# Linear attention and two MLPs on one core: eight slots for input weights, out weights laid out by result

## The chip, the cores and the metric

The program runs on one core of one Trainium2 chip. The metric is its time on the chip in microseconds (us), as the median of several runs. TensorE (PE) multiplies, ScalarE (ACT), VectorE (DVE) and GpSimd (POOL) work on elements, SyncE (SP) issues most of the transfers.

## The reference, cut to what matters

Four batches of eight heads, 576 positions, head size 64: linear attention, then two MLPs over the 2304 tokens, all with a model size of 512. In the kernel's inputs the values are 64 bits wide; the kernel turns the weights into 32-bit numbers itself.

```python
def phi(x):
    proj = np.einsum('bhsd,df->bhsf', x, w_phi)               # 64 -> 128
    proj = proj - np.max(np.abs(proj), axis=-1, keepdims=True)
    return np.concatenate([np.exp(proj), np.exp(-proj)], axis=-1)
kv = np.einsum('bhsf,bhsd->bhfd', phi(k), v)
attn = (phi(q) @ kv) / (phi(q) @ z + 1e-06)                   # z: sum of phi(k)
x = attn                                                      # 2304 x 512
h = x @ w_in                                                  # 512 -> 2048
x = np.maximum(0.01 * h, h) @ w_out                           # 2048 -> 512
g = x @ w_gate                                                # 512 -> 1536
out = (g * (1 / (1 + np.exp(-g))) * (x @ w_val)) @ w_out2     # 1536 -> 512
```

## The kernel before, in words

**Products.** Each factor of a product is split into a high and a low part, and a product is three matmuls: high by high, high by low, low by high. A weight tile is 128 x 2 x 512: 512 columns of the high part and 512 of the low one. Results stand in four PSUM banks ("pm"), 128 x 288 each, half of a batch's 576 tokens.

**Units.** The MLPs are cut into 297 units, in order of the batches 0 to 3 (`units`). In the first two batches a unit is 24 matmuls (two halves of 12): `u_l1` (one 128-wide block f of the first MLP's 2048 columns), `u_gate` and `u_val` (the same for the second MLP's 1536), and `u_out`. `u_out(kind, b, c, o)` multiplies four blocks of such columns (a chunk c of `CH` = 4) by the out weights and adds the product to result block o, one of four (`KD`). A chunk's four `u_out` follow when its blocks are there. The addition on VectorE (L883) frees the PSUM bank. In the third batch's first MLP (`seven_beside`) and in the whole fourth batch (`seven`) two first-layer products are made with seven block products where eight are usual (class `Quad`), and `u_out` comes in halves beside them.

**Weights.** A weight tile has a key (kind, batch, number); the kinds are "1" (w_in), "2" (w_out), "g", "v" and "3" (w_out2). In the first batch a key is a raw 64-bit load of 512 KB into a slot of tag "wi" (`w_load`, L675; five slots of 4 KB a partition), a conversion to 32 bits into tag "wr" (four slots; `f32_steps`, ScalarE L691 to L697, VectorE L701 to L719), and a split into a high and a low part (`to_wtile`: ScalarE L737, VectorE L78). The split tile of a first-layer key is in "wi" too, that of an out key in "wo" (five slots). Results are stored to memory: 32-bit weights as `kept` (SyncE, L725), split out weights as `parts` (by GpSimd's queue, L773, 28 of them). The second batch loads `kept` again and splits again, the later ones load `parts` (L656). In the fourth batch the out tile whose number is 3 modulo 4 has a slot of its own ("vhl").

**What sets the order.** The lists `need` and `after` say when a key is due: a first-layer key has its slot four units ahead of the unit that needs it, an out key right after the unit that makes the columns it multiplies. `order` is the list of all keys by slot. For each key `split_next` (L1228) loads two keys past those done, converts one past, splits one, and then loads on up to `depth()` keys past those done: 5, or 4 where a key of batch 1 is near. All loads stand in SyncE's queue, where one that has no slot yet holds back those behind it.

**Attention.** That of the first batch is the opening, an order written out by hand (`OPENING`, some 450 names; CG3 and CG2 are steps of the conversion of the third kind of the first four weights, KP11 a product of the keys, XL7 the last result's low part). At KP2 in it the first four raw weights are loaded. The attention of each later batch is spread over the units of the one before. A scheduler of the language makes the final order of each engine of all this.

The out weights of key ("2", b, f) before are rows 128 f to 128 f + 127 of w_out, for all four results: the 512 columns of its tile are four blocks o of 128, and `u_out` takes block `oc` of four tiles.

Of the kernel before, what the change touches and what calls it, by code (L numbers as in the profile page):

```python
# [60 lines left out]
def linear_attention_two_mlps(ctx: ExitStack, tc, qT, kT, vt, w_phi, w1, w2, wg, wv, w3, cst, out):  # L61
# [573 lines left out]
    def parts_tile(key):  # L635
        tag = ("wi", 5)
# [21 lines left out]
    def w_load(key, tag="wi", n=5):  # L658
# [6 lines left out]
        elif (kind, f) in parts and second_of_pair(key):  # L665
            d = parts[kind, f].rearrange("p (a k n) -> p a k n", a=2, k=2)
            tag = ("wr", 4) if kind == "1" else ("wi", 5)
# [88 lines left out]
    def w_split(key):  # L756
# [20 lines left out]
        if kind == "1":  # L777
# [5 lines left out]
            for name, x in (("1X", even), ("1Y", r)):  # L783
                t = T([P, 2, 512], F32R, "wi", 5)
                to_wtile(t, x)
                unkept.append(((name, f // 2), t))
# [284 lines left out]
    after = {}  # L1071
# [17 lines left out]
    def seven(kind, b):  # L1089
# [5 lines left out]
        def o():  # L1095
            if not queue:
                return lambda: None
            (k, bb, c, last), oo, t = queue.pop(0)
            return lambda: u_out(k, bb, c, oo, last, (t,))

        def all_of(*fns):
            return lambda: [fn() for fn in fns]

# [10 lines left out]
        for m in range(n):  # L1114
# [15 lines left out]
            if kind == "1":  # L1130
                for f in range(4 * m, 4 * m + 4):
                    after.setdefault(end, []).append(("2", b, f))
                held.append(("1", b, m, m == n - 1))
            elif m % 2:
                for f in range(2 * m - 2, 2 * m + 2):
                    after.setdefault(mid, []).append(("3", b, f))
# [9 lines left out]
    def seven_beside(b):  # L1146
# [4 lines left out]

        def o():
            (k, bb, c, last), oo, t = queue.pop(0)
            return lambda: u_out(k, bb, c, oo, last, (t,))

        def two(*fns, w=()):
            return unit(lambda: [fn() for fn in fns], w)
# [4 lines left out]
        for m in range(NF1 // 4):  # L1162
# [10 lines left out]
            places = [two(y.p5, more[1]), two(more[2], more[3])]  # L1173
            two(more[4], more[5])
            places.append(two(more[6], y.p3))
            end = two(more[7], y.p4, w=[("1", b, 4 * m + 3)])
            places.append(end)
            for k in range(4):
                after.setdefault(places[k] if m == 0 else end, []).append(("2", b, 4 * m + k))
# [5 lines left out]
    for b in range(QB):  # L1185
        first = len(units)
        for f in range(NF1 if b != QA else 0):
            unit(lambda b=b, f=f: u_l1(b, f), [("1", b, f)])
            flush()
            after.setdefault(len(units) - 1, []).append(("2", b, f))  # L1190
# [6 lines left out]
        for f in range(NF2):  # L1197
# [3 lines left out]
            after.setdefault(len(units) - 1, []).append(("3", b, f))  # L1201
# [9 lines left out]
    for i in range(NU):  # L1211
        for k in need[i]:
            slots[max(-1, i - 4)].append(k)
        slots[i] += after.get(i, [])
# [138 lines left out]
```

## Time and profile before

| | |
|---|---|
| median of 3 runs | 1054.92 us (1054.34 to 1055.16) |
| the profiled execution | 1054.82 us |
| its span, first to last instruction | 1052.9 us |
| TensorE busy, matmuls | 1036.7 us, 98% |
| VectorE busy | 793.5 us, 75% |
| ScalarE busy | 650.5 us, 62% |
| GpSimd busy | 21.4 us, 2% |

The profile is one execution. Busy is the time in which an engine has an instruction in work; matmuls overlap each other, so that a busy share says when TensorE stands still, and not how well it is used. A line such as L816 is a line of the kernel; `pm<-gp,wo` reads: tile pm written from tiles gp and wo.

### The profile page before, as it was taken

To read this page: it belongs to the slowest core of one execution; us is meant where nothing else is said; L and a number is where in the kernel's file an instruction comes from. 1 tells how busy PE (TensorE), PEld (TensorE's weight loads), DVE (VectorE), ACT (ScalarE), POOL (GpSimd) and SP (SyncE) were. 2 spreads that over 40 slices of the span, in tenths; PEclk is the share of its full clock that TensorE was granted. 3 is DMA by queue.
4 is the path that set the end of the run, shared out by engine and by line. 5 is a ranking of instruction groups with operands and counts; after the bars stand their busy time and mean duration, and the time that the engine had idled before them with its cause. 6 is when DMAs were issued, how large, how long until landed. Compare 5 with 4: busy or idle time off the path is not lost.

```text
span 1052.9 us, 20402 instructions
## 1 busy us (share of the span) xinstructions
PE 1036.7 (98%) x7638; PEld 1016.8 (97%) x7638; DVE 793.5 (75%) x1726; ACT 650.5 (62%) x1448; POOL 21.4 (2%) x57
## 2 busy tenths in 40 slices
PE   9999999999999999999999999999999999999998
PEld 7899999999999999999999989999999999999998
DVE  6988888998999799678676766868778632468464
ACT  6879887898977788456543667735443244336431
POOL 1001100000000000000000000000000000000000
PEclk9999999999999999999999999999999999999999
DMA  8239777577765998765535486356886777558542
GB/s 267 60 129 309 274 264 263 168 248 217 261 192 200 356 339 284 285 230 192 192 120 189 134 319 243 141 203 217 291 285 237 272 267 264 183 167 297 191 145 76
DMA packets 101489, 236.16 MB, mean 224 GB/s; under 512 B 19856, under 2 KB 35984, under 8 KB 101392
## 3 DMA queue, kind: packets, MB, share of 16 engines
q1 hardware_dynamic: 95888, 219.74, 60.3%
q0 software_dynamic: 4032, 14.68, 3.6%
q8 instruction: 60, 0.98, 0.4%
q10 hardware_dynamic: 1472, 0.46, 0.2%
q14 instruction: 37, 0.30, 0.1%
HBM read 169.30 MB, written 65.54 MB: 223 GB/s over the span
## 4 chain that ended last, share of the span: by engine, by line
PE 83%; DVE 6%; ACT 5%; DMA 4%; issue 1%; SPq 0%; POOL 0%; DVEq 0%; ACTq 0%; POOLq 0%
PE pm L816 55%; PE pa L942 9%; PE pm L942 5%; PE pa L459 5%; PE pa L248 2%; PE pa L260 2%; PE pa L207 2%; DMA wi<-in_w_dram 2%; ACT wr L691 1%; DMA wr<-kept 1%; ACT wi L694 1%; ACT gp L90 1%; DVE gp L78 1%; PE pm L518 1%; DVE wr L701 1%
## 5 line engine op out<-in xcount | busy, mean ns | idle before, releaser
L816 PE MATMUL pm<-xh,wi 128*128 128x288 f32 x1664 | 350.5, 298 | 1.4 <-ACT wi L737 1.2
L816 PE MATMUL pm<-gp,wo 128*128 128x288 f32 x2256 | 338.4, 296 | 2.8 <-DVE acc L883 2.3
L816 PEld LDWEIGHTS pm<-gp,wo 128*128 128x128 f32 x2256 | 311.9, 188 | 4.8 <-DVE acc L883 3.0
L816 PEld LDWEIGHTS pm<-xh,wi 128*128 128x128 f32 x1664 | 271.1, 188 | 3.2 <-ACT wi L737 1.4
L816 PE MATMUL pm<-xl,wi 128*128 128x288 f32 x832 | 246.2, 297 | 0.0
L816 PEld LDWEIGHTS pm<-xl,wi 128*128 128x128 f32 x832 | 156.1, 188 | 0.8
L883 DVE TENSOR_TENSOR acc<-pm,acc 128x288 f32<-128x288 f32 x160 | 70.0, 452 | 47.2 <-PE pm L816 46.4
L78 DVE TENSOR_TENSOR gp<-es,gp 128x576 fp32r<-128x576 f32 x94 | 70.6, 752 | 31.8 <-ACT gp L90 31.0
L90 ACT ACTIVATE gp<-es 128x576 fp32r<-128x576 f32 x94 | 64.8, 694 | 29.9 <-DVE es L864 24.9
L78 DVE TENSOR_TENSOR wi<-wr,wi 128x512 fp32r<-128x512 f32 x96 | 64.7, 683 | 12.1 <-ACT wi L737 11.5
L737 ACT ACTIVATE wi<-wr 128x512 fp32r<-128x512 f32 x92 | 58.0, 643 | 25.6 <-PE pm L816 10.8
L942 PE MATMUL pm<-xh,wi 128*128 128x288 f32 x272 | 62.6, 297 | 1.8 <-DMA wi<-parts 1.6
L78 DVE TENSOR_TENSOR fl<-ff,fh 128x512 fp32r<-128x512 f32 (+1 forms) x72 | 50.9, 712 | 12.1 <-ACT fh L90 11.8
L691 ACT ACTIVATE wr<-wi 128x512 f32<-128x512 f32 x68 | 47.9, 704 | 17.0 <-DMA wi<-in_w_dram 7.8
L719 DVE TENSOR_TENSOR wr<-wr,wi 128x512 uint16<-128x512 uint16 x68 | 51.1, 754 | 0.8
L942 PEld LDWEIGHTS pm<-xh,wi 128*128 128x128 f32 x272 | 46.3, 188 | 2.9 <-DMA wi<-parts 1.8
L694 ACT ACTIVATE wi<-wi 128x512 int32<-128x512 uint32 x68 | 47.8, 703 | 0.0
L90 ACT ACTIVATE fh<-ff 128x512 fp32r<-128x512 f32 (+1 forms) x72 | 47.2, 665 | 0.8
L844 ACT ACTIVATE es<-pm 128x288 f32<-128x288 f32 x72 | 29.8, 431 | 25.4 <-PE pm L942 15.9
L465 ACT ACTIVATE dn<-pa 64x288 f32<-64x288 f32 x64 | 26.0, 407 | 30.5 <-PE pa L459 29.5
L90 ACT ACTIVATE acc<-pm 128x288 f32<-128x288 f32 x64 | 26.7, 433 | 26.3 <-PE pm L816 26.0
L864 DVE SCALAR_TENSOR_TENSOR es<-pm,es 128x288 f32<-128x288 f32 x72 | 32.1, 449 | 14.3 <-PE pm L816 14.1
(214 smaller groups left out, 2068.0 us busy)
## 6 DMA issues: line engine op xcount, KB each, us to landing
wo<-parts SPq DMA_DIRECT2D x77, 512.0 KB, 6.2
wi<-parts SPq DMA_DIRECT2D x68, 512.0 KB, 5.6
parts<-wi SPq DMA_DIRECT2D x56, 512.0 KB, 4.9
wi<-in_w_dram SPq DMA_DIRECT2D x44, 512.0 KB, 5.0
wr<-kept SPq DMA_DIRECT2D x64, 256.0 KB, 4.8
parts<-wo POOLq DMA_DIRECT2D x28, 512.0 KB, 5.2
kept<-wr SPq DMA_DIRECT2D x40, 256.0 KB, 4.5
wi<-in_wg_dram SPq DMA_DIRECT2D x12, 512.0 KB, 4.6
```

The costliest lines, as they stand in the source:

```text
L78: keep(dve.tensor_tensor(out=o, in0=a, in1=b, op=ALU.subtract))
L90: keep(act.activation(o, a, AF.Copy))
L459: keep(pe.matmul(ps, w, x, start=(i == 0), stop=(i == len(ops) - 1)))
L691: after_opening(act.activation(t[0], high.bitcast(F32), AF.Abs, scale=REBIAS))
L694: after_opening(act.activation(low, low.bitcast(U32), AF.Copy, scale=2.0**-29))
L719: keep(dve.tensor_tensor(out=t16, in0=t16, in1=e16, op=ALU.add))
L737: i = act.activation(t[:, 0], r, AF.Copy)
L816: m = pe.matmul(ps, w, x[:, c], start=(i == 0), stop=(i == n - 1))
L844: act.activation(o, i, AF.Prelu, alpha=0.01)
L864: dve.scalar_tensor_tensor(out=g[:, c], in0=ps, scalar=0.5, in1=g[:, c], op0=ALU.mult, op1=ALU.mult)
L883: dve.tensor_tensor(out=acc[o][:, t], in0=ps, in1=acc[o][:, t], op=ALU.add)
L942: m = pe.matmul(ps, a, b, start=start and n == 0, stop=stop and n == 5, skip_group_check=True)
```

## The change

It has four parts. (1) GpSimd's area for descriptors is 2048 bytes where it was 16384 by default, and tag "wi" has eight slots where it had five. (2) In the opening, at CG3 and at CG2, two more raw weights each are loaded. (3) w_out and w_out2 are laid out by result: tile `KD * c + o` holds, for result o, the four blocks of 128 rows of chunk c side by side. `u_out` takes all its weights from one tile (`out_key`), and an out key is now due like a first-layer key, four units ahead of the unit that needs it; `after` is gone. (4) `depth()` is 8, or 4 where one of the next six keys is of batch 1.

```diff
     def parts_tile(key):
-        tag = ("wi", 5)
+        tag = ("wi", 8)
         if key[0] in "23":
             tag = ("vhl", 1) if key[1] == QB and key[2] % CH == CH - 1 else ("wo", 5)
...
+    def out_key(kind, b, c, o):
+        return "2" if kind == "1" else "3", b, KD * c + o
+
     def u_out(kind, b, c, o, last, halves=(0, 1)):
         ops = []
-        oc = slice(P * o, P * o + P)
-        for f in range(CH * c, CH * c + CH):
-            w = wtile["2" if kind == "1" else "3", b, f]
-            h, l = w[:, 0], w[:, 1]
-            a, d = gp[kind, b, f]
-            ops += [(h[:, oc], a), (h[:, oc], d), (l[:, oc], a)]
+        w = wtile[out_key(kind, b, c, o)]
+        h, l = w[:, 0], w[:, 1]
+        for n in range(CH):
+            r = slice(P * n, P * n + P)
+            a, d = gp[kind, b, CH * c + n]
+            ops += [(h[:, r], a), (h[:, r], d), (l[:, r], a)]
...
         for o in range(KD):
-            unit(lambda o=o: u_out(kind, b, c, o, last))
+            unit(lambda o=o: u_out(kind, b, c, o, last), [out_key(kind, b, c, o)])
...
             unit(lambda b=b, f=f: u_l1(b, f), [("1", b, f)])
             flush()
-            after.setdefault(len(units) - 1, []).append(("2", b, f))
...
     def depth():

-        nxt = order[done[0] + 2 : done[0] + 5]
-        return 4 if any(k[1] == 1 for k in nxt) else 5
+        nxt = order[done[0] + 2 : done[0] + 8]
+        return 4 if any(k[1] == 1 for k in nxt) else 8
...
         if name == "KP2":
             load_q(0, 3)
             ahead(loaded, w_load, 4)
+        if name in ("CG3", "CG2"):
+            ahead(loaded, w_load, loaded[0] + 2)
...
+    def rows(w):
+        return w.reshape(-1, CH, P, KD, P).transpose(0, 3, 2, 1, 4).reshape(-1, P, 512)
...
-        "w2": inputs["moe_w_out"].reshape(NF1, P, DM),
+        "w2": rows(inputs["moe_w_out"]),
...
-        "w3": inputs["moe2_w_out"].reshape(NF2, P, DM),
+        "w3": rows(inputs["moe2_w_out"]),
...
-    nc = _bacc.Bacc("TRN2", target_bir_lowering=False, num_devices=1)
+    nc = _bacc.Bacc("TRN2", target_bir_lowering=False, num_devices=1, dynamic_dma_scratch_size=2048)
```

What is left out does the same at the other places: the slots of "wi" in `w_load` and `w_split`, and, in `seven` and `seven_beside`, a list `late` that hands the key of each first half of `u_out` to its unit's needs in place of `after`. The number of instructions of every engine stays as it was; their order is new in most of the program. Three places follow.

SyncE in the opening, before: kept are stores of converted weights, pk and raw loads of values and keys for the attention, wi loads of raw weights (number 201 on are the fifth weight on, an out weight first).

```order
L725 DMA kept_94_398<-wr_71_318 128x512
L167 DMA pk_165_646<-in_vt_dram 128x2x64
L725 DMA kept_114_480<-wr_60_274 128x512
L167 DMA pk_241_939<-in_vt_dram 128x4x64
L167 DMA pk_242_942<-in_vt_dram 128x4x64
L725 DMA kept_150_601<-wr_82_348 128x512
L675 DMA wi_201_778<-in_w2_dram 128x1024
L155 DMA raw_240_937<-in_kT_dram 128x576
L675 DMA wi_202_780<-in_w1_dram 128x1024
L675 DMA wi_208_801<-in_w2_dram 128x1024
```

The same place of the change:

```order
L725 DMA kept_94_398<-wr_71_318 128x512
L167 DMA pk_169_654<-in_vt_dram 128x2x64
L675 DMA wi_105_439<-in_w1_dram 128x1024
L675 DMA wi_106_441<-in_w2_dram 128x1024
L725 DMA kept_116_484<-wr_60_274 128x512
L167 DMA pk_240_932<-in_vt_dram 128x4x64
L167 DMA pk_241_935<-in_vt_dram 128x4x64
L725 DMA kept_152_605<-wr_82_348 128x512
L675 DMA wi_156_615<-in_w2_dram 128x1024
L675 DMA wi_157_617<-in_w2_dram 128x1024
L155 DMA raw_239_930<-in_kT_dram 128x576
```

Four raw loads now stand ahead of loads and stores that were ahead of them, in two pairs, and the first of them is a first-layer weight (w1) where it was an out weight (w2).

SyncE where the third batch begins, before: `parts` are split weights in memory, the stores at L895 those of the second batch's results, vraw a load of values for the last attention. Tile wi_1641 is the first of the three loads issued at 603.11.

```order
L895 DMA out_0_dram<-acc_1380_6723 128x576
L895 DMA out_0_dram<-acc_1395_6790 128x576
L656 DMA wi_1600_7873<-parts_936_4544 128x1024
L656 DMA wr_1603_7904<-parts_899_4369 128x2x256
L656 DMA wo_1604_7906<-parts_207_799 128x1024
L656 DMA wr_1626_7987<-parts_930_4506 128x2x256
L895 DMA out_0_dram<-acc_1413_6862 128x576
L174 DMA vraw_1708_8345<-in_vt_dram 128x640
L656 DMA wo_1635_8034<-parts_225_872 128x1024
L656 DMA wi_1641_8056<-parts_993_4822 128x1024
```

The same place of the change, where the load of that weight (parts_993) goes to wi_1639 and the first store of a result has moved to L898:

```order
L656 DMA wi_1588_7774<-parts_935_4542 128x1024
L656 DMA wr_1592_7807<-parts_899_4369 128x2x256
L656 DMA wo_1624_7983<-parts_883_4300 128x1024
L656 DMA wr_1633_8030<-parts_930_4506 128x2x256
L656 DMA wi_1639_8052<-parts_993_4822 128x1024
L656 DMA wi_1640_8054<-parts_1030_4977 128x1024
L898 DMA out_0_dram<-acc_1380_6723 128x576
```

The weight's load stood behind three stores of results, the load of values and one more load of an out tile than now; it has moved ahead of all the stores.

TensorE, half of an out unit in the third batch's first MLP, before (gp, mrow and pk hold the columns of the first layer, wo the out weights):

```order
L816 MATMUL pm_9466<-gp_8900,wo_8986 128x288 x3
L816 MATMUL pm_9466<-mrow_8945,wo_9036 128x288
L816 MATMUL pm_9466<-pk_8946,wo_9036 128x288
L816 MATMUL pm_9466<-mrow_8945,wo_9036 128x288
L816 MATMUL pm_9466<-gp_9126,wo_9066 128x288 x3
L816 MATMUL pm_9466<-gp_9153,wo_9068 128x288 x3
```

The same half unit in the change:

```order
L816 MATMUL pm_9478<-gp_8902,wo_9074 128x288 x3
L816 MATMUL pm_9478<-mrow_8949,wo_9074 128x288
L816 MATMUL pm_9478<-pk_8950,wo_9074 128x288
L816 MATMUL pm_9478<-mrow_8949,wo_9074 128x288
L816 MATMUL pm_9478<-gp_9132,wo_9074 128x288 x3
L816 MATMUL pm_9478<-gp_9159,wo_9074 128x288 x3
```

Four weight tiles have become one.

## Rows read from the trace of the kernel before

**Rows 1.** The page: span, engines, busy tenths by slice (26.3 us), two matmul groups.

```profile
span 1052.9 us, 20402 instructions
...
PE 1036.7 (98%) x7638; PEld 1016.8 (97%) x7638; DVE 793.5 (75%) x1726; ACT 650.5 (62%) x1448; POOL 21.4 (2%) x57
...
DVE  6988888998999799678676766868778632468464
...
DMA  8239777577765998765535486356886777558542
...
L816 PE MATMUL pm<-xh,wi 128*128 128x288 f32 x1664 | 350.5, 298 | 1.4 <-ACT wi L737 1.2
L816 PE MATMUL pm<-gp,wo 128*128 128x288 f32 x2256 | 338.4, 296 | 2.8 <-DVE acc L883 2.3
```

**Rows 2.** The chain that ended last, first and last: start, us, work.

```profile
1.10 2.93 PE pm L135 x6
...
1036.35 12.75 PE pm L816 x96
```

**Rows 3.** TensorE by time: start, us, work, in brackets the idle before it.

```profile
82.39 0.41 PE L816 MATMUL pm<-xh,wi 128*128 128x288 f32 x1 [1.18 <-ACT wi L737]
...
122.22 1.06 PE L816 MATMUL pm<-gp,wo 128*128 128x288 f32 x6 [0.33 <-DVE gp L78]
...
189.78 3.71 PE L816 MATMUL pm<-gp,wo 128*128 128x288 f32 x26 [1.75 <-DVE acc L883]
...
226.13 1.24 PE L459 MATMUL pa<-ff,kvh 128*128 128x288 f32 x4 [0.70 <-ACT ff L436]
...
599.75 1.76 PE L816 MATMUL pm<-gp,wo 128*128 128x288 f32 x12
...
607.76 0.40 PE L942 MATMUL pm<-xh,wi 128*128 128x288 f32 x1 [1.57 <-DMA wi<-parts]
...
698.59 0.63 PE L816 MATMUL pm<-mrow,wo 128*128 128x288 f32 x3 [0.71 <-DMA wo<-parts]
...
933.70 0.37 PE L816 MATMUL pm<-ff,vhl 128*128 128x288 f32 x1 [0.79 <-DMA vhl<-parts]
```

**Rows 4.** The chain again, landings of raw weights ahead of three waits: start, us.

```profile
112.23 7.25 DMA wi<-in_w_dram
...
171.32 4.54 DMA wi<-in_wv_dram
...
216.51 4.20 DMA wi<-in_w_dram
```

**Rows 5.** SyncE's queue by time: issues of transfers.

```profile
70.14 1.75 SPq L675 DMA_DIRECT2D wi<-in_w_dram  x4
...
75.76 0.33 SPq L155 DMA_DIRECT2D raw<-in_kT_dram  x1
...
603.11 1.38 SPq L656 DMA_DIRECT2D wi<-parts  x3
```

**Rows 6.** TensorE by time: first uses of two attention tiles.

```profile
96.01 0.60 PE L207 MATMUL pa<-wbd,raw 128*128 128x256 f32 x2
...
147.16 1.06 PE L248 MATMUL pa<-pk,ff 96*128 96x128 f32 x8
```

**Rows 7.** GpSimd by time.

```profile
105.30 0.31 POOL L165 MEMSET pk<- 128x256 f32 x1 [7.37 <-PE pa L248]
...
111.53 1.74 POOL L773 DMA_DIRECT2D parts<-wo  x3 [5.25 <-DVE wo L78]
```

**Rows 8.** Busy time of each engine in one stretch.

```profile
core 0: us, PE busy (x) PEld busy (x) DVE busy (x) ACT busy (x) POOL busy (x), PEclk, DMA share, GB/s
...
79.00:105.30 26.30, 24.69 (x185) 23.86 (x184) 22.93 (x49) 26.30 (x71) 2.74 (x8) 1.00 0.90 309
```

**Rows 9.** VectorE by line: out<-in, times, busy us, mean ns, idle before.

```profile
L701 DVE SCALAR_TENSOR_TENSOR wr<-wr,wi 128x512 int32<-128x512 int32 x40 | 27.3, 682 | 4.6 <-ACT wi L697 4.0
```

**Rows 10.** Waits of SyncE's queue: in all, times, the longest.

```profile
SPq L656 <- PE pm L816: 155.2, 58, 21.1
```

More of the change, by code (lines that the diff above doesn't have):

```diff
@@ L656, in in_turn, with w_load @@
         tc.stamp_issue_order_token(nc.sync.dma_start(out=o, in_=i).ins, "loads")
-    def w_load(key, tag="wi", n=5):
+    def w_load(key, tag="wi", n=8):
         kind, b, f = key
@@ L666, in w_load @@
             d = parts[kind, f].rearrange("p (a k n) -> p a k n", a=2, k=2)
-            tag = ("wr", 4) if kind == "1" else ("wi", 5)
+            tag = ("wr", 4) if kind == "1" else ("wi", 8)
             wtile[key] = t = T([P, 2, 256], F32R, *tag)
@@ L783, in w_split @@
             for name, x in (("1X", even), ("1Y", r)):
-                t = T([P, 2, 512], F32R, "wi", 5)
+                t = T([P, 2, 512], F32R, "wi", 8)
                 to_wtile(t, x)
@@ L1070, in linear_attention_two_mlps @@
     units, need = [], []
-    after = {}
     def unit(fn, w=()):
@@ L1098, in o, with unit @@
             (k, bb, c, last), oo, t = queue.pop(0)
+            if t == 0:
+                late.append(out_key(k, bb, c, oo))
             return lambda: u_out(k, bb, c, oo, last, (t,))
+        late = []
         def all_of(*fns):
             return lambda: [fn() for fn in fns]
+        def unit(fn, w=()):
+            units.append(fn)
+            need.append(list(w) + late)
+            late.clear()
+            return len(units) - 1
         src_x = (xh, xl) if kind == "1" else (x2h, x2l)
@@ L1130, in seven @@
             if kind == "1":
-                for f in range(4 * m, 4 * m + 4):
-                    after.setdefault(end, []).append(("2", b, f))
                 held.append(("1", b, m, m == n - 1))
             elif m % 2:
-                for f in range(2 * m - 2, 2 * m + 2):
-                    after.setdefault(mid, []).append(("3", b, f))
                 held.append(("3", b, m // 2, m == n - 1))
@@ L1150, in seven_beside @@
         held.clear()
+        late = {}
         def o():
             (k, bb, c, last), oo, t = queue.pop(0)
-            return lambda: u_out(k, bb, c, oo, last, (t,))
+            fn = lambda: u_out(k, bb, c, oo, last, (t,))
+            if t == 0:
+                late[fn] = out_key(k, bb, c, oo)
+            return fn
         def two(*fns, w=()):
-            return unit(lambda: [fn() for fn in fns], w)
+            return unit(lambda: [fn() for fn in fns], list(w) + [late[fn] for fn in fns if fn in late])
         two(o(), o())
@@ L1172, in seven_beside @@
             two(x.p4, more[0], w=[("1", b, 4 * m + 1)])
-            places = [two(y.p5, more[1]), two(more[2], more[3])]
+            two(y.p5, more[1])
+            two(more[2], more[3])
             two(more[4], more[5])
[L1175 to L1179, printed above, removed]
+            two(more[6], y.p3)
+            two(more[7], y.p4, w=[("1", b, 4 * m + 3)])
             if m < NF1 // 4 - 1:
@@ L1200, in linear_attention_two_mlps @@
             unit(lambda b=b, f=f: u_val(b, f), [("v", b, f)])
-            after.setdefault(len(units) - 1, []).append(("3", b, f))
             if f % CH == CH - 1:
@@ L1213, in linear_attention_two_mlps @@
             slots[max(-1, i - 4)].append(k)
-        slots[i] += after.get(i, [])
     order = [k for i in range(-1, NU) for k in slots[i]]
```

## The prediction

> **What bounds the kernel now.** I read the page first, then the chain of waits, then TensorE by time for every stretch in which it stood still, then, for each of these, the queue or engine that it waited for. The page says that TensorE (PE) is busy for 1036.7 us of a span of 1052.9 [rows 1], so it stands still for 16.2 us. The chain begins with its first matmul at 1.10 and ends with its last at 1036.35 + 12.75 = 1049.10 [rows 2]: 1.1 us ahead, 3.8 us behind, and so 11.3 us in the middle. The change leaves the number and shape of the matmuls as they are, so that what it can win lies in these 11.3 us and in what belongs to them. A wait costs a little more than its shown idle: twelve matmuls take 1.76 us from the start of the first to the end of the last and one takes 0.298 [rows 1, 3], so that they follow each other every (1.76 - 0.298) / 11 = 0.133 us; the one before a wait shows busy for 0.298 where 0.133 would have passed. I add 0.16 us to each wait.
>
> Four of the waits in the middle are for a weight tile [rows 3]: at 82.39 (1.18 us, for ScalarE's split), and for the landing of a direct load at 607.76 (1.57), 698.59 (0.71) and 933.70 (0.79). Three more, at 122.22 (0.33), 189.78 (1.75) and 226.13 (0.70), are put down to an engine, but the chain that leads to each of them begins with the landing of a raw weight: loads of 7.25, 4.54 and 4.20 us, behind which ScalarE and VectorE stand [rows 4]. These seven make 7.03 of the 11.3 us.
>
> **The change, part by part.** *Instructions.* Their counts are the same on every engine. The out matmuls now take their weights from one tile where they took them from four. A first-layer matmul has always taken them from one, and lasts 298 ns against 296 [rows 1]; I cost this at nothing. 24 matmuls make a unit of 24 x 0.133 = 3.2 us.
>
> *Late tiles, term A.* At 82.39 the fifth first-layer weight is late since its conversion stood behind those of four out weights that were due later. Now it is the first after the opening, and its raw load and three others are issued within the opening. At 607.76 the load was issued at 603.11 at the earliest, some 4.6 us before the wait ended [rows 3, 5], since the queue's head had waited for slots. Three more slots let about three keys more stand loaded, which is 3 x 3.2 = 9.6 us, against 1.57 that were missing. At 698.59 all four out tiles that a chunk needs were released only with the last result of the chunk before; one tile per result lets them go one by one, a result (3.2 us) apart, against 0.71. At 933.70 one tile in a slot of its own was needed by every result of a chunk, first by the first one; now it serves the last result alone, which is three results (9.6 us) later, against 0.79. All four go: 4.25 + 4 x 0.16 = **4.9 us**. What would be late next behind these loads is ScalarE's split, which the first rival takes up.
>
> *Raw loads, term B.* The three waits that begin with a raw landing end 0.33 to 1.75 us late. The loads are issued three keys, 9.6 us, earlier than they were, which is more than the longest of them lasts (7.25). Their worth lies between 0 (if the conversions on ScalarE and VectorE are as late without the load) and 2.78 + 3 x 0.16 = 3.3 us. I take **3.3**, since the missing amounts are a fraction of the lead.
>
> *Four loads in the opening.* Four raw loads take SyncE (SP) 1.75 us to issue [rows 5], in two pairs, so what stands behind a pair is 0.9 us later. The next attention load behind them, of keys at 75.76, is used by TensorE first at 96.01 [rows 5, 6]: its lead of 20.3 us covers that. The DMA engines read 2 and 3 tenths busy in the second and third slice, 26 to 79 us, and 9 in the fourth [rows 1]; loads that move from the fourth to these fall where there is room. Cost nothing; without this cover 0.9 us.
>
> *GpSimd's descriptor area, cut to an eighth.* Only stores of split out weights go by GpSimd's queue. Three of them are issued in 1.74 us [rows 7], 0.58 each. No row shows what a full area does. From below it costs nothing; from above each store would wait for the landing of the one before, about 4.5 us (the raw loads of the same size took 4.20 and 4.54 [rows 4]). Then a memset behind three stores would be some 14 us late. The memset at 105.30 fills a tile that TensorE first reads at 147.16 [rows 7, 6], 41.9 us later, so that even the upper bound is covered. I take nothing. The Trainium skill ("DMA: Bandwidth & Descriptors", section "Why small descriptors are slow (HBM only)") gives 16 bytes for a descriptor to read and 16 for one to write: by it 2048 bytes would hold some 128 of a kind (an estimate), which no row here shows to bind or not to bind.
>
> *What the new order brings.* Every weight's place in the order changes, and a scheduler lays out each engine's queue anew, so some new small waits will appear. From below none; from above one burst like the two longest of the old ones, 1.57 + 1.75 + 0.32 = 3.6 us. I take five (one in each of: the two MLPs of the first batch, the passage into the third batch, the first MLP of the third, the last batch) of the smallest size in the rows, 0.33 + 0.16 = 0.49: **2.5 us**.
>
> **Sum.** The profiled execution took 1054.82 us, 1.9 more than its span and 0.1 less than the median of the three runs. 1054.82 - 4.9 - 3.3 + 2.5 = 1049.1 us. Ends of this case: with A and B in full and nothing new 1046.6; with A alone and the burst 1054.82 - 4.9 + 3.6 = 1053.5. A measurement can tell some 0.2% from no change, 2.1 us; faster means below 1052.8, slower above 1057.0.
>
> **Rivals.** *1. The conversions bound the first batch, so that the earlier loads win nothing there.* For it: ScalarE is busy for 26.30 of 26.30 us between 79.00 and 105.30 [rows 8], and VectorE reads 9 tenths in four of the nine slices of the first batch [rows 1]. The wait at 82.39 and term B then stay, shorter loads or not, and only the three late direct loads go: 1.57 + 0.71 + 0.79 + 3 x 0.16 = 3.55. 1054.82 - 3.55 + 2.5 = 1053.8: no change that can be told. The same comes out if the extra slots stay empty because SyncE's queue stands for other reasons. Against it: each of the three chains of term B begins with a landing, not with an engine's backlog. A rule goes further. TensorE's weight loads are busy for 97% of the span [rows 1]. The Trainium skill ("Perfetto Trace Analysis", section "Identifying the Most-Contended Engine") says to judge TensorE by its weight loads' busy share and to optimize the most contended engine first; a change that leaves all its work as it is would by this rule give nothing, 1054.8. The trace agrees on which engine it is, and its 11.3 us of idle bound what the change can win to 1.1%. Chance 0.12.
>
> *2. VectorE takes TensorE's place, and the kernel gets slower.* With one key to each unit, a conversion now also stands beside the out units, where few did, ahead of the additions that free TensorE's result banks. One such operation takes 0.68 us [rows 9]. The first batch has 40 additions (24 + 16, from the loops); four of nine slices with VectorE at 9 tenths hold some 18, and if half of these find a conversion ahead that TensorE can't cover, 9 x 0.68 = 6.1 us are lost. 1054.82 - 3.55 + 6.1 = 1057.4. It decides where VectorE's backlog ahead of an addition is longer than the work in the three other banks, 3 x 12 x 0.133 = 4.8 us. For it: at 189.78 TensorE did wait 1.75 us for such an addition [rows 3]. Against it: the sum of VectorE's work is the same, and the conversions are spread more evenly than before. Chance 0.07.
>
> *3. The loads that run ahead block SyncE's queue for the attention's loads.* A weight's load that has no slot holds back everything behind it; the longest such wait was 21.1 us [rows 10]. If one of these now stands ahead of a load with the lead of 20.3 us, and the load takes 4.5 us to land [rows 4], TensorE waits 21.1 + 4.5 - 20.3 = 5.3 once, with 0.16 more: 1049.1 + 5.5 = 1054.6, no change. Against it: more slots make such waits shorter, and the out tiles come free one by one. Chance 0.05.
>
> **How the numbers follow.** The forecast case has 0.76, of which 0.02 lies above 1052.8. Faster by over 0.2%: 0.74. Within 0.2%: 0.02 + 0.12 + 0.05 = 0.19. Slower: 0.07, the second rival. The predicted time is that of the forecast, 1049.1. The forecast's own range, 1046.6 to 1053.5, holds less than the chance wanted, so that the range goes up over the first rival, to 1054.4, and at the low end takes in one more small wait that may go, to 1046.2.
>
> **What would show it.** In TensorE by time: no wait for a weight's load or split near 82, 607, 698 and 933, none at 122, 190 and 226 whose chain begins with a raw landing; idle of TensorE at about 10.5 us in the span where it was 16.2. In SyncE by time: two pairs of raw loads in the opening, and around 600 us weight loads ahead of the first store of a result. On the page: DMA's second and third tenths up. The forecast is wrong if waits for VectorE's additions (rival 2) or for attention loads (rival 3) have come instead, or if the waits of the first batch are as long with their loads landed early (rival 1).

## The result and the profile after

The change took 1045.16 us by the median of 6 runs (1044.78 to 1046.10), the kernel before 1055.04 (6 runs beside it); the ratio is 0.990, 95% interval 0.988 to 0.992. The forecast was 1049.1 with a range from 1046.2 to 1054.4. The direction was right; the gain is 9.9 us where 5.8 were forecast, and the time lies 1.0 us below the range.

The page of the kernel after, with the lines that answer to [rows 1]: span and busy time of the engines, then two groups of matmuls.

```profile
span 1044.3 us, 20425 instructions
...
PE 1035.1 (99%) x7638; PEld 1017.0 (97%) x7638; DVE 791.9 (76%) x1726; ACT 648.1 (62%) x1448; POOL 21.7 (2%) x57
...
L816 PE MATMUL pm<-xh,wi 128*128 128x288 f32 x1664 | 349.8, 297 | 0.2 <-ACT es L844 0.2
L816 PE MATMUL pm<-gp,wo 128*128 128x288 f32 x2172 | 328.8, 297 | 0.4 <-DVE acc L886 0.2
```

TensorE does the same matmuls and stands still less: 1044.3 - 1035.1 = 9.2 us where it was 16.2, 7.0 of the 8.6 us by which the span is shorter. The other 1.6 is that it is busy for less (1035.1 against 1036.7): nine waits fewer behind the opening, at the 0.16 that the prediction adds to each, would be 1.4. The out matmuls with one weight tile last 297 ns, with four they lasted 296 [rows 1]: cost nothing, as said.

To see where the time went I cut the program at three small waits that every version has: after the opening, near the end of the second batch, and in the fourth batch. TensorE by time, kernel before (start, us, work, idle before it):

```profile
66.41 0.41 PE L816 MATMUL pm<-xh,wi 128*128 128x288 f32 x1 [0.24 <-ACT es L844]
...
586.26 0.40 PE L816 MATMUL pm<-gp,wo 128*128 128x288 f32 x1 [0.23 <-DVE acc L883]
...
949.24 0.40 PE L942 MATMUL pa<-xh,kvl 128*128 128x288 f32 x1 [0.50 <-ACT raw L90]
```

The same three in the kernel after, and between them the three largest waits that it still has:

```profile
67.45 0.40 PE L816 MATMUL pm<-xh,wi 128*128 128x288 f32 x1 [0.23 <-ACT es L844]
...
72.35 0.35 PE L248 MATMUL pa<-pk,ff 128*128 128x128 f32 x1 [0.67 <-issue]
...
188.30 0.40 PE L366 MATMUL pa<-pk,wst_h 128*128 128x288 f32 x1 [0.40 <-ACT ff L436]
...
582.72 0.40 PE L816 MATMUL pm<-gp,wo 128*128 128x288 f32 x1 [0.22 <-DVE acc L886]
...
610.39 0.39 PE L207 MATMUL pa<-wbd_h,pk 128*128 128x256 f32 x1 [0.41 <-ACT kvz L90]
...
940.34 0.40 PE L945 MATMUL pa<-xh,kvl 128*128 128x288 f32 x1 [0.50 <-ACT raw L90]
```

None of the seven waits of [rows 3] is left at its place; the one at 188.30 has the same releaser (ScalarE's exponentials, L436) as that at 226.13 had, for another matmul. The *first stretch* (67 to 583 us, nearly all of the MLPs of the first two batches) went from 519.85 to 515.27, 4.58 less. The *second stretch* (the passage into the third batch, the third batch, the start of the fourth) went from 362.98 to 357.62, 5.36 less. The opening was 1.04 longer and the end 0.30: 4.58 + 5.36 - 1.04 - 0.30 = 8.6 us, the difference of the spans. The opening varied by 0.5 us in an execution of the same instructions as before (its mark stood at 66.94 in the run with the small descriptor area alone) and by 0.75 in one of the change itself (66.70), so its 1.04 is mostly not the change's.

### The profile page after: what moved, and what is told of

Same layout as the page of the kernel before. It is cut to its first block, busy times and chain, and to the rows that moved or that the text cites. A ratio compares the mean times of both kernels' runs of the same rounds, so it can differ in the third digit from the quotient of the medians.

```text
span 1044.3 us, 20425 instructions
## 1 busy us (share of the span) xinstructions
PE 1035.1 (99%) x7638; PEld 1017.0 (97%) x7638; DVE 791.9 (76%) x1726; ACT 648.1 (62%) x1448; POOL 21.7 (2%) x57
## 4 chain that ended last, share of the span: by engine, by line
PE 90%; ACT 4%; DVE 3%; DMA 2%; issue 1%; SPq 0%; ACTq 0%
PE pm L816 61%; PE pa L945 9%; PE pm L945 6%; PE pa L459 5%; PE pa L248 2%; PE pa L207 2%; PE pa L260 2%; DMA xl<-in_vt_dram 1%; ACT wr L691 1%; ACT wi L694 1%; DMA wi<-in_w_dram 1%; PE pa L367 1%; PE pa L366 1%; PE pa L420 1%; DVE xl L78 1%
## 5 line engine op out<-in xcount | busy, mean ns | idle before, releaser
L816 PE MATMUL pm<-gp,wo 128*128 128x288 f32 x2172 | 328.8, 297 | 0.4 <-DVE acc L886 0.2
L816 PEld LDWEIGHTS pm<-gp,wo 128*128 128x128 f32 x2172 | 301.1, 188 | 1.9 <-ACT acc L90 0.5
L886 DVE TENSOR_TENSOR acc<-pm,acc 128x288 f32<-128x288 f32 x160 | 70.6, 451 | 47.8 <-PE pm L816 47.1
L691 ACT ACTIVATE wr<-wi 128x512 f32<-128x512 f32 x68 | 47.5, 699 | 10.5 <-DVE wi L78 4.2
L694 ACT ACTIVATE wi<-wi 128x512 int32<-128x512 uint32 x68 | 47.7, 702 | 0.0
```

What stands on the lines that cost most here:

```text
L691: after_opening(act.activation(t[0], high.bitcast(F32), AF.Abs, scale=REBIAS))
L694: after_opening(act.activation(low, low.bitcast(U32), AF.Copy, scale=2.0**-29))
L816: m = pe.matmul(ps, w, x[:, c], start=(i == 0), stop=(i == n - 1))
L886: dve.tensor_tensor(out=acc[o][:, t], in0=ps, in1=acc[o][:, t], op=ALU.add)
```

## The experiments

Twelve more runs were made; the last two repeat a kernel. The table gives each median with the ratio to the kernel before on the same chip, and the two stretches, from one execution each.

| kernel | median, us | ratio, 95% interval | first stretch | second stretch |
|---|---|---|---|---|
| before | 1055.04 | 1 | 519.85 | 362.98 |
| the change | 1045.16 | 0.9898 (0.9875 to 0.9922) | 515.27 | 357.62 |
| layout and due times alone | 1049.02 | 0.9936 (0.9914 to 0.9958) | 519.02 | 358.06 |
| slots and depth alone | 1051.87 | 0.9967 (0.9954 to 0.9980) | 516.09 | 364.23 |
| slots and loads in the opening | 1052.38 | 0.9970 (0.9957 to 0.9982) | 516.29 | 366.13 |
| the change without those loads | 1043.35 | 0.9888 (0.9867 to 0.9909) | 513.30 | 357.65 |
| descriptor area alone | 1054.63 | 0.9997 (0.9981 to 1.0012) | 519.09 | 362.30 |
| without those loads, depth 5 | 1049.63 | 0.9956 (0.9941 to 0.9972) | 519.44 | 358.80 |
| without those loads, six slots | 1047.30 | 0.9934 (0.9921 to 0.9947) | 517.09 | 357.65 |
| the change, pair at CG3 alone | 1044.09 | 0.9905 (0.9890 to 0.9921) | 513.29 | 357.65 |
| layout alone, due as before | 1052.62 | 0.9975 (0.9961 to 0.9989) | 521.26 | 358.82 |
| the change, pair at CG2 alone | 1044.28 | 0.9892 (0.9872 to 0.9911) | 513.39 | 358.11 |
| the change, again | 1045.28 | 0.9899 (0.9882 to 0.9917) | 515.01 | 357.61 |
| without those loads, again | 1044.08 | 0.9891 (0.9872 to 0.9910) | 513.29 | 360.43 |

Two things have to be known to read the stretches. One is how much they vary. With the descriptor area alone the instructions and their order are those of the kernel before, and the stretches are 0.76 and 0.68 us shorter; the second execution without the loads in the opening has a second stretch 2.8 longer than the first.

The other is TensorE's clock. In three of these executions the granted clock falls to the lower of its two levels, 1.2 GHz, behind long waits: behind 1.91 us at 204.08 (depth 5), behind 0.62 and 0.95 us at 180.95 and 182.43 (six slots) and behind 1.78 us at 932.08 (slots and loads in the opening). For depth 5, busy time in two stretches (TensorE, its weight loads, VectorE, ScalarE, GpSimd; then the granted clock, the DMA engines' share and GB/s):

```profile
204.00:205.00 1.00, 0.92 (x7) 0.92 (x8) 1.00 (x4) 1.00 (x4) 0.00 (x0) 1.00 0.76 207
...
206.00:207.00 1.00, 1.00 (x6) 1.00 (x6) 0.80 (x2) 1.00 (x3) 0.00 (x0) 0.50 0.00 0
```

From 205.25 to 208.61 fourteen matmuls follow each other every 0.24 us where 0.133 is usual, which loses 3.36 - 14 x 0.133 = 1.5 us; the other two executions lose about as much (an estimate). Not every long wait brings it: behind 1.75 us in the kernel before and 1.66 with the slots alone the clock stayed at 1.00.

### The parts one by one

**Layout and due times alone**: the change without its slots, depth, loads in the opening and descriptor area.

```diff
-        tag = ("wi", 8)
+        tag = ("wi", 5)
...
-        nxt = order[done[0] + 2 : done[0] + 8]
-        return 4 if any(k[1] == 1 for k in nxt) else 8
+        nxt = order[done[0] + 2 : done[0] + 5]
+        return 4 if any(k[1] == 1 for k in nxt) else 5
...
-        if name in ("CG3", "CG2"):
-            ahead(loaded, w_load, loaded[0] + 2)
```

> The layout by result and its due times alone: five slots for input weights, depth 5, no loads in the opening, the descriptor area as before. Theory (each part removes its own waits): the waits near 82, 698 and 933 us go (1.18 + 0.71 + 0.79 + 3 x 0.16 = 3.2 us), the one near 607 stays and so do most of those at 122, 190 and 226: 1054.8 - 3.2 = 1051.6 us by one execution. Rival A (slots alone do it): no change, 1054.8, since without slots no load can run ahead. Rival B (the even order of one key to each unit does it all): all seven waits go, 1046.2.

Measured 1049.02, better than the theory, and rival A falls. Nearly all of the second stretch's gain is there with five slots: 358.06, 4.92 of 5.36. The wait near 607, which the theory had left to the slots, is gone, and so are those near 122 and 226. The first stretch gained only 0.8, no more than it varies, so that rival B's 1046.2 is not reached either: the wait near 190 is still there, and others came:

```profile
188.82 0.40 PE L816 MATMUL pm<-gp,wo 128*128 128x288 f32 x1 [1.07 <-DVE acc L886]
...
317.99 0.37 PE L816 MATMUL pm<-xh,wi 128*128 128x288 f32 x1 [0.35 <-DVE es L857]
319.10 0.40 PE L816 MATMUL pm<-xh,wi 128*128 128x288 f32 x1 [0.61 <-DVE wi L78]
...
352.62 0.40 PE L816 MATMUL pm<-xh,wi 128*128 128x288 f32 x1 [1.07 <-ACT wi L737]
```

**Slots and depth alone**: the kernel before with eight slots, the new `depth()` and the small descriptor area.

```diff
-        tag = ("wi", 5)
+        tag = ("wi", 8)
...
-        nxt = order[done[0] + 2 : done[0] + 5]
-        return 4 if any(k[1] == 1 for k in nxt) else 5
+        nxt = order[done[0] + 2 : done[0] + 8]
+        return 4 if any(k[1] == 1 for k in nxt) else 8
```

> Eight slots, depth 8 and the smaller descriptor area alone; out weights laid out and due as before, no loads in the opening. Theory: the wait near 607 (1.57 + 0.16) and those at 122, 190 and 226 (3.3) go; those near 82, 698 and 933 stay, since the four out tiles and the slot of their own are released as before: 1054.8 - 5.0 = 1049.8 us. Rival A: all of the gain, 1046.2. Rival B: nothing, 1054.8.

Measured 1051.87, between the theory's 1049.8 and rival B's 1054.8. The first stretch gained 3.76, and the wait near 82, which the theory had left in place, is gone; the second stretch lost 1.25. TensorE by time shows that the late tiles of the second stretch are all still late; that at 931 is worse than before:

```profile
604.38 0.40 PE L942 MATMUL pm<-xh,wi 128*128 128x288 f32 x1 [1.60 <-DMA wi<-parts]
...
695.05 0.37 PE L816 MATMUL pm<-mrow,wo 128*128 128x288 f32 x1 [0.47 <-DMA wo<-parts]
...
931.57 0.37 PE L816 MATMUL pm<-ff,vhl 128*128 128x288 f32 x1 [1.66 <-DMA vhl<-parts]
```

SyncE's queue of this kernel says why three more slots did nothing for the first of them. By time, then its waits between 585 and 606 us (in total, times, longest):

```profile
594.82 0.34 SPq L174 DMA_DIRECT2D vraw<-in_vt_dram  x1
599.33 0.33 SPq L656 DMA_DIRECT2D wo<-parts  x1
599.71 1.37 SPq L656 DMA_DIRECT2D wi<-parts  x3
```

```profile
SPq L174 <- DVE vhl L78: 6.8, 1, 6.8
SPq L656 <- PE pm L816: 4.1, 1, 4.1
```

The tile that TensorE waits for is loaded by the first of the three at 599.71, and ahead of it in the queue stand an attention load that waited 6.8 us and an *out* tile that waited 4.1 us for its slot in "wo". The out tile's wait ended last, so that it is what the load waited for in the end. A slot in "wi" is of no use to a load that can't get to the head of the queue. From the mark of the second batch's end the load is as late as before (599.71 - 582.89 = 16.82 us; before 603.11 - 586.26 = 16.85). With the layout alone the same weight is the first of three loads that begin at 595.16:

```profile
595.16 3.53 SPq L656 DMA_DIRECT2D wi<-parts  x3
```

That is 595.16 - 586.29 = 8.9 us behind the mark; with layout and slots it is ahead of all of the second batch's result stores and so ahead of the mark, the kernel after:

```profile
570.28 3.84 SPq L656 DMA_DIRECT2D wi<-parts  x2
...
583.05 0.34 SPq L898 DMA_DIRECT2D out_dram<-acc  x1
```

**The loads in the opening**, added to the slots alone, and taken from the change.

```diff
+        if name in ("CG3", "CG2"):
+            ahead(loaded, w_load, loaded[0] + 2)
```

> As the run before with the four raw loads in the opening added, out weights laid out and due as before. Theory: the fifth key stays fifth in the order, and the wait near 82 is for its conversion behind four others, so the loads alone win at most a part of its 1.18 us: 1049 to 1049.8. Rival A: 1046.2. Rival B: 1054.8. If the loads in the opening are what removes the waits of the first batch, this run is better than the one before by the waits at 82, 122, 190 and 226, up to 4.6 us.

> The whole change without the four raw loads in the opening. Theory: the fifth key is now first in the order, so its conversion is late only if its load is; issued after the opening, at about 70 us, it lands about 5 us later, and the wait near 82 goes or is short: 1046.2 to 1047.4 us. Rivals A and B: 1046.2, the loads are hidden anyway. If the opening's loads carry the first batch: 1046.2 + up to 4.6 = 1050.8.

They win nothing. On the slots alone the time is 1052.38, above the theory's 1049.8, and the first stretch is 516.29 against 516.09 without them (the second, 366.13, has the lower clock at 933 to 936 us in this execution, so I compare only the first). Without them the change is *faster*: 1043.35, and 513.30 in the first stretch. The loads are hidden anyway: even without them the scheduler lets two raw loads out at 51.64 us, and six more from 70.97 on, and TensorE has no wait for one. What was not expected is that the change loses 2 us by them. The next runs look at this.

### What the loads in the opening cost

Two runs keep one pair each.

```diff
-        if name in ("CG3", "CG2"):
+        if name == "CG3":
             ahead(loaded, w_load, loaded[0] + 2)
```

> The whole change with the loads at CG2 left out and those at CG3 kept: two raw loads in the opening. Theory (the loads in the opening win nothing, and what the full change lost against the run without them is a few waits of a freshly built order): anywhere from 1043 to 1046 us, with the waits at other places than in the full change. Rival (each pair has a price of its own, in SyncE's queue or on the DMA engines): half way, 1044.3 us, with the full change's waits near 72 and 188 us, shorter.

> The whole change with the loads at CG3 left out and those at CG2 kept. Theory (a load in the opening has no price of its own, and the 2 us that the full change lost between 67 and 583 us against the runs with one pair or none belong to its own order of conversions and attention): 1043 to 1044.5 us, 513.3 us in that stretch. Rival (the pair at CG2 is what costs, as the run with the pair at CG3 alone lost nothing): 1045.2 us, 515.3 in that stretch.

Either pair alone leaves the first stretch at 513.3 or 513.4, so neither pair has a price of its own; both rivals fall. The change and the run without the loads were run once more beside each other:

> The change itself, beside the run without its loads in the opening on the same chip. Theory: its 515.3 us between 67 and 583 us, with waits near 72 and 188 us, come back within 0.7 us, 1045.2 us by the median. Rival (that stretch varies by 2 us from one execution to the next): 513.3 to 514, and no wait near 188.

> The change without its loads in the opening, once more on the chip that runs the change beside it. Theory: 1.5 to 2 us faster than the change, 1043.4. Rival: within 0.7 us of it.

The change has 515.01 again, with waits at 71.57 (0.64) and 187.30 (0.37) in the places of 72.35 and 188.30. The run without the loads came out 1.2 us faster by the median, between the 1.5 that the theory wanted and the rival's 0.7. The loss in the first stretch is there again, and belongs to what the scheduler makes of two pairs. ScalarE by time shows how. The kernel after:

```profile
67.58 0.45 ACT L90 ACTIVATE xh<-xf 128x288 fp32r<-128x288 f32 x1
67.92 0.67 ACT L691 ACTIVATE wr<-wi 128x512 f32<-128x512 f32 x1
...
71.30 0.69 ACT L691 ACTIVATE wr<-wi 128x512 f32<-128x512 f32 x1
71.86 0.39 ACT L218 ACTIVATE ff<-pa,mn 128x128 f32<-128x128 f32 x1
```

With the pair at CG3 alone:

```profile
67.25 0.45 ACT L90 ACTIVATE xh<-xf 128x288 fp32r<-128x288 f32 x1
67.58 0.67 ACT L691 ACTIVATE wr<-wi 128x512 f32<-128x512 f32 x1
...
69.27 0.68 ACT L694 ACTIVATE wi<-wi 128x512 int32<-128x512 uint32 x1
69.84 0.36 ACT L218 ACTIVATE ff<-pa,mn 128x128 f32<-128x128 f32 x1
```

Seven conversion steps (67.92 to 71.86; the five rows left out alternate between L694 and L691) stand ahead of the attention's exponentials (L218), where four stand there with one pair (two rows left out). TensorE's L248, which multiplies what these write, then waits 0.67 us at 72.35; with one pair it doesn't wait. (The profile names no releaser there, only "issue"; I take it to be L218, which ends at 71.86 + 0.39 = 72.25, just ahead.) The loads themselves hold nothing up; with more weights *ready* by then the scheduler puts more conversions ahead of work that TensorE needs sooner. It goes by how many raw loads SyncE issues between 30 and 55 us: four in the two executions of the change and in the two with the slots under the old layout, all with this wait (0.64 to 0.67); two in the six executions with the layout, more than five slots and one pair or none; one in the four with five slots; none of these ten has it. The slots alone bring four without any line in the opening. SyncE's queue, with the slots alone, then in the change without the loads:

```profile
51.77 1.82 SPq L675 DMA_DIRECT2D wi<-in_w_dram  x4
```

```profile
51.64 0.87 SPq L675 DMA_DIRECT2D wi<-in_w_dram  x2
```

So it is the scheduler's choice, and the two pairs only one way to bring it about. At 188.30 the wait is again for ScalarE's exponentials (L436); its cause I did not follow as far. The two with what each costs beyond its idle (0.16 each) are 1.4 us, but the versions with at most one pair have a wait of 0.38 to 0.44 near 94 that the change lacks: waits explain some 0.8 of the 2.0 us. In the rest TensorE is busy, for longer with the same number of matmuls, and why is open. The first stretch of the change, then without the loads:

```profile
67.45:582.72 515.27, 513.74 (x3830) 507.61 (x3830) 441.58 (x936) 382.22 (x861) 17.12 (x35) 1.00 0.69 241
```

```profile
66.67:579.97 513.30, 512.66 (x3830) 507.32 (x3830) 442.40 (x936) 383.56 (x861) 17.31 (x35) 1.00 0.68 244
```

By medians the version without the loads is the fastest that ran (1043.35 and 1044.08, against 1045.16 and 1045.28 for the change); beside each other on one chip the runs overlap (1043.44 to 1046.42 and 1044.72 to 1046.38), so that I rest the claim on the first stretch: 513.29 to 513.39 in four executions with at most one pair, 515.01 and 515.27 in two with both.

### Slots, depth, due times, descriptor area

**Depth and number of slots**, both without the loads in the opening.

```diff
-        nxt = order[done[0] + 2 : done[0] + 8]
-        return 4 if any(k[1] == 1 for k in nxt) else 8
+        nxt = order[done[0] + 2 : done[0] + 5]
+        return 4 if any(k[1] == 1 for k in nxt) else 5
```

> Layout and eight slots, no loads in the opening, but depth() as before (5, or 4 near batch 1). Theory (the loads must run further ahead, and slots that the order does not fill are worth nothing): the waits of the layout alone come back in the first batch, about 1048 to 1050 us. Rival (the free slots themselves let a load go out without waiting for a conversion, whatever the depth): as with layout and slots, 1043 to 1044.5.

```diff
-        tag = ("wi", 8)
+        tag = ("wi", 6)
...
-        nxt = order[done[0] + 2 : done[0] + 8]
-        return 4 if any(k[1] == 1 for k in nxt) else 8
+        nxt = order[done[0] + 2 : done[0] + 6]
+        return 4 if any(k[1] == 1 for k in nxt) else 6
```

> Layout and six slots with depth 6, no loads in the opening: one slot more than before in place of three. Theory (each slot gives about 3.2 us of lead, and raw loads take 4 to 7): part of the way between the layout alone (1049.0) and layout with eight slots (1043.4), about 1046. Rival (the first slot more is enough, since the missing amounts are under 2 us): 1043.4 to 1044.4.

Eight slots that the order doesn't fill win nothing that can be told: with depth 5 the time is 1049.63 (with five slots 1049.02) and the first stretch 519.44 (519.02), of which some 1.5 is the lower clock. Six slots with depth 6 give 517.09, about 515.6 without the lower clock, and eight 513.30. By the ratios six are not told from five (0.9934 and 0.9936), and the time, 1047.30, is above the theory's 1046; eight are clear of both (0.9888). Depth 8 with five slots was not run. In the runs with depth 5 and with six slots the second stretch has its 358.8 and 357.65; it doesn't care for slots once the layout is there. What is left with too little lead are waits for VectorE and ScalarE, not for a landing; here the longest of the run with depth 5, and then of that with six slots:

```profile
204.08 0.40 PE L816 MATMUL pm<-xh,wi 128*128 128x288 f32 x1 [1.91 <-DVE es L857]
```

```profile
182.43 0.56 PE L816 MATMUL pm<-gp,wo 128*128 128x288 f32 x1 [0.95 <-DVE gp L78]
```

**The layout alone, with the keys due as before**: `u_out` takes one tile, and nothing else is changed.

```diff
+        w = wtile[out_key(kind, b, c, o)]
+        h, l = w[:, 0], w[:, 1]
+        for n in range(CH):
+            r = slice(P * n, P * n + P)
+            a, d = gp[kind, b, CH * c + n]
+            ops += [(h[:, r], a), (h[:, r], d), (l[:, r], a)]
...
-        "w2": inputs["moe_w_out"].reshape(NF1, P, DM),
+        "w2": rows(inputs["moe_w_out"]),
```

> The layout by result alone, and the out keys due as before, right after the unit that makes the columns: no need four units ahead, five slots, depth 5. Theory (the gain of some 5 us behind 586 us comes from out tiles that come free one result after the other): the stretch from the wait near 586 us to the one near 949 takes 358 us as in the run with the layout and its due times, where it took 363 before: about 1049.8 us. Rival (the gain comes from the due times, which spread the loads evenly over the units): 363 us there, 1054.8.

The second stretch is 358.82: that out tiles come free one result after the other gives 4.2 of its 5.4 us by itself. Ahead of the third batch's first weight the out tile still stands in SyncE's queue, but the tile goes out without a wait, and the attention load now stands behind:

```profile
596.56 0.43 SPq L656 DMA_DIRECT2D wo<-parts  x1
597.09 3.48 SPq L656 DMA_DIRECT2D wi<-parts  x3
600.66 0.38 SPq L174 DMA_DIRECT2D vraw<-in_vt_dram  x1
```

No run changes only one of the two. The time, 1052.62, is above the theory's 1049.8, because the first stretch lost 1.4 (521.26). There the due times matter: with them (the layout run, still five slots) it is 519.02. The wait for the fifth weight's split is back, as large as before:

```profile
82.86 0.40 PE L816 MATMUL pm<-xh,wi 128*128 128x288 f32 x1 [1.16 <-ACT wi L737]
```

Either cure is enough for it: it is gone in the run with the layout and its due times, and in the one with the slots alone.

**The descriptor area alone.**

```diff
-    nc = _bacc.Bacc("TRN2", target_bir_lowering=False, num_devices=1)
+    nc = _bacc.Bacc("TRN2", target_bir_lowering=False, num_devices=1, dynamic_dma_scratch_size=2048)
```

> The kernel before with GpSimd's descriptor area at 2048 bytes and nothing else. Theory (the area costs nothing): the same program at the same time, ratio 1.000 within 0.2%, and GpSimd's stores still issued in 0.5 to 0.7 us each. Rival: the smaller area holds the stores up, so that GpSimd's memsets come late: slower, by up to some 1 us for each late memset that TensorE waits for.

It costs nothing that can be told: 0.9997 (0.9981 to 1.0012). GpSimd's stores by line (times, busy us, mean ns, idle before them), before and then with the small area:

```profile
L773 POOL DMA_DIRECT2D parts<-wo x28 | 15.0, 536 | 236.8 <-DVE wo L78 208.8 <-PE pa L248 25.6 <-DVE top L394 1.1
```

```profile
L773 POOL DMA_DIRECT2D parts<-wo x28 | 15.1, 538 | 236.0 <-DVE wo L78 197.5 <-PE pa L248 25.6 <-DVE es L857 9.9
```

## Why the prediction was right, and where it was wrong

**Right: the bound, the seven waits, and that they end on the side forecast.** TensorE remains the bound, and all seven waits of terms A and B are gone. Their 4.9 + 3.3 = 8.2 us are near the 8.6 by which the span fell, but that is partly luck, as the next paragraphs show. Of the signs, the two pairs of loads and the weight loads ahead of the result stores came; TensorE's idle is 9.2 where about 10.5 was named. DMA's second and third tenths read 2 and 3 as before; only the GB/s of the page rose there, from 60 to 98 and from 129 to 145.

**Wrong: the term for the new order, 2.5 us of new waits.** This is the step that failed. I took five new waits for five places. The second stretch has no more waits than it had (at 610.39 stands one of 0.41 where one of 0.44 stood at 613.50), and two small ones that I had left in place went (0.40 at 752.93, 0.24 at 948.21): it gained 5.36 where term A gave 1.57 + 0.71 + 0.79 + 3 x 0.16 = 3.55, 1.8 more. These two are 1.0 of the 1.8; the other 0.8 no wait shows. The first gained 4.58, just what A and B have there (1.18 + 0.16 + 3.3 = 4.6); its two new waits (1.07 idle) are for the most part paid for by two old ones that went, at 80.00 (0.43) and 287.34 (0.33). In that stretch a gain of 1.9 more than A and B and a loss of 2.0 by the loads in the opening cancel (both below). So the term was about -1.8 where I took +2.5, and part of this came back by the opening and the end (1.04 + 0.30). 2.5 + 1.8 - 1.3 = 3.0 us of the miss are this; the other 0.9 is that the profiled execution of the change, 1046.10, is the slowest of its six. The error of judgement behind it: I counted what a new order may break and not what it may mend.

**Wrong in its cause: the wait near 607.** I put it down to slots in "wi". The slots alone leave 1.60 us of it, the layout alone removes it: the load was held behind an out tile that waited for a slot in "wo" in the same queue, and behind an attention load. For 698 and 933 the cause was as given: they stay with the slots alone and go with the layout (that at 933 was missing once without it, with the descriptor area alone).

**Term B, 3.3: a cause that holds, and a size met by luck.** Slots give it, and only if the depth fills them: 3.8 us of the first stretch by slots alone (with 82's wait in it), nothing that can be told by eight slots with depth 5. But layout and slots together give 6.55 (519.85 - 513.30), more than the two apart (0.83 + 3.76); that the due times spread the conversions, and the loads are then early enough to use that, is my reading and not shown apart. The change has 4.58 because the loads in the opening took 2.0 of the 6.55 back: two errors that cancel. Nor is 2.78 a fixed sum of idle: with the descriptor area alone the waits near 122, 190 and 226 are none, 0.97 and 0.30.

**Wrong: the loads in the opening cost nothing.** I costed their issue, and asked what stood behind them in SyncE's queue. I did not ask what their landing would release: conversions ahead of the attention's exponentials on ScalarE. With both pairs the first stretch is 2.0 us longer, of which that wait is 0.83.

**The descriptor area and the one-tile matmuls** cost nothing, as said.

**The rivals.** The first fell. ScalarE was even fuller, in the stretch where it was to be the bound; busy time between 70 and 120 us (TensorE, its weight loads, VectorE, ScalarE, GpSimd), before and after:

```profile
70.00:120.00 50.00, 48.39 (x363) 47.25 (x362) 42.15 (x85) 46.58 (x118) 6.25 (x15) 1.00 0.88 302
```

```profile
70.00:120.00 50.00, 49.23 (x369) 48.06 (x368) 45.22 (x93) 49.71 (x127) 6.28 (x14) 1.00 0.85 296
```

A full ScalarE was not a late one: with its loads landed it did more of its work in this stretch (127 instructions against 118), and TensorE stood still less. The 1054.8 beside this rival was my reading of a rule of the Trainium skill ("Perfetto Trace Analysis", "Identifying the Most-Contended Engine"): optimize the most contended engine first. TensorE's weight loads have the same 97% of a span that is 8.6 us shorter, so that the measurement decides against that reading. The rule itself does not say that work left as it is gives nothing: the same page of the Trainium skill goes on, under "Optimization Strategy", to look for that engine's gaps and what blocks it there, and says that one gap that keeps coming back can mean too little room for the next tile. The gaps here were single ones, and the runs with five, six and eight slots still point that way (first stretch 519.0, 517.1 and 513.3 us). The second rival (VectorE's additions) appears only where the lead is short: 1.07 us for L886 with the layout alone, 0.51 with depth 5; the change has 0.22, its mark at 582.72. The third did not come: behind the opening TensorE has no wait for a load.

## What to carry to other kernels

When a load is late, read what stands ahead of it in its queue before adding buffers for it: here a tile of another kind, waiting for its own slot, held it back, and giving each tile one consumer (so that slots come free one by one) won 4.2 us in the stretch where three more slots won nothing. Buffers count only if the issue order runs far enough ahead to fill them. And a load that comes earlier is not free because it is hidden: ask which work becomes ready with it, and what that work will stand in front of.

## What the runs showed that was not expected

Waits at the same place vary by about a microsecond from one execution to the next. The kernel with the small descriptor area has the same instructions in the same order as before; at the places of the waits at 189.78 (1.75) [rows 3] and 287.34 (0.33) it shows:

```profile
188.94 0.40 PE L816 MATMUL pm<-gp,wo 128*128 128x288 f32 x1 [0.97 <-DVE acc L883]
...
287.11 0.40 PE L816 MATMUL pm<-gp,wo 128*128 128x288 f32 x1 [1.23 <-DVE acc L883]
```

In the second execution of the version without the loads, VectorE waited 4.27 us for one load of a kept weight, and TensorE, behind VectorE, 1.63; in the first execution VectorE's wait there was 0.47 and TensorE had none. VectorE and TensorE by time, second execution, then VectorE in the first:

```profile
739.12 0.43 DVE L792 TENSOR_TENSOR wr<-wr 128x256 f32<-128x256 f32 x1 [4.27 <-DMA wr<-kept]
...
740.27 0.40 PE L816 MATMUL pm<-gp,wo 128*128 128x288 f32 x1 [1.63 <-DVE gp L78]
```

```profile
734.97 0.43 DVE L792 TENSOR_TENSOR wr<-wr 128x256 f32<-128x256 f32 x1 [0.47 <-DMA wr<-kept]
```

The transfer decides the second case; for the first no run tells the cause. One trace shows one draw.

The kernel before also spreads more than the change: 1052.95 to 1060.24 in the six runs beside it, where the change has 1044.78 to 1046.10. TensorE's clock goes with this. Of the 57 runs of the kernel before beside the experiments, 27 have a mean granted clock of 0.999 or 1.000, with a median of 1053.87 us, and 30 have 0.998 or less, with a median of 1056.5. All 31 runs of the versions with the layout, eight slots and depth 8 have 0.999 or more. That the longer runs of the kernel before have the lower clock behind one of its long waits fits the three executions above but is not shown: no execution of it with a lowered clock has a trace. If it is so, a long wait can cost more than its idle and the 0.16 us that the prediction adds, and the medians credit the change with that too: against 1053.87 it is 8.7 us faster in place of 9.9, which is what the spans of the two profiled executions say (8.6).
